# The early order of a fused attention and feed-forward kernel, laid out anew from the third scores to the first layer

## The chip, the cores and the metric

One core of a Trainium2 chip runs the kernel. The metric is the device time of one execution in microseconds; the median of three runs of the kernel before is 292.87 us (292.86 to 293.62).

## The reference

Inputs: `q`, `k`, `v` of 4 batches, 8 heads, 768 positions, 64 features; a projection to 6 hash bits; a norm gain; two weight matrices of 512 x 2048 and 2048 x 512.

```
q_bits = (einsum('bhsd,dk->bhsk', q, proj) > 0)
k_bits = (einsum('bhsd,dk->bhsk', k, proj) > 0)
mask = q_bucket[:, :, :, None] == k_bucket[:, :, None, :]
scores = where(mask, scale * q @ k^T, -1e9)
attn = softmax(scores)
x = (attn @ v), heads side by side: 4 x 768 x 512
xn = (x - mean(x)) / sqrt(var(x) + 1e-6) * g_ln
out = x + relu(xn @ w_ch1) @ w_ch2
```

## The kernel before

The work is cut into 12 units `u` of 256 query positions (three to a batch), and each unit into two groups `g` of 4 heads. A score block `s` is a unit, a group and a third of the keys (`kp`, 256 keys): `s = 6u + 3g + kp`, so there are 72.

Nothing is scheduled by a compiler. The string `ORDER` lists 1186 words; each word calls one function, and its second part names the engine that runs it: `t` TensorE (PE), `v` VectorE (DVE), `a` ScalarE (ACT), `p` GpSimd (POOL), `s` SyncE (SP, which issues most transfers). Each engine runs its words in the order of the string, and waits for what its operands and its buffers need. The string `SLOTS` names for each ring of buffers (a tag) which buffer each new tile takes, in the order in which tiles first appear; a new tile in a buffer must wait until the old one there has been read. The PSUM rings are `pp` (three buffers, for scores `sc` and for the sums `acc`) and `f` (two buffers, for everything else that PE writes).

The words that matter here, with the function's lines:

- `S.t.s` (L570): 24 small matmuls of one score block, 32 rows each, first the hash signs `G`, then the two halves of the features (`qb`, `kb`), into two `sc` tiles. `E.a.s.h` (L576): the exponential of half a block, 128 x 1024.
- `A.t.s` (L595): 16 matmuls of 65 columns, exponentials by values, added into `acc` of the unit and group. `na.v.u.g` (L608) reads `acc` when its three blocks are in; `nb` (L615, L617) divides; `nc`, `ag`, `ce` (L621 to L630) make the norm.
- For batch 0 the blocks of q and k are turned on DVE in thirds (`tn.v.g.t.kp`, L304; `t` is 0 for q, 1 for k), cast (`ca`, L311 to L315), hashed on PE (`ha`, L394, or by `hc`, `sl`, L405 and L418) and cut to signs (`bh`, `bc`, L307, `bi`, L428 and L430).
- For batch 1 and later a block of q or k is loaded by `LX.s.b.g.t` (L508) once `gx.p.b.g.t` (L505) has written one element of its buffer, a memset that stands for the wait until the buffer is free. `tu.v.b.g.t.n` (L304) turns a quarter of it, `CA` casts it, `hm.t.b.g` (L526) hashes all of q and k of a group once all eight `tu` are in, `bt` (L307) cuts to signs, and `mw` and `mr` (L544, L547) take them through DRAM.
- `ft.t`, `fc.v` (L644, L652) transpose unit 0's rows by PE and scale them. `F.t.u.p` (L659) is a first-layer block: 8 matmuls of 256 columns for two of the 16 hidden blocks. `R` (L667 on ACT, L669 on DVE) is its relu. `D.t` (L674) is the second layer of unit 0; later units use `P`, `Y` (L726, L731).
- `lw1.p.n`, `lw2.p.n` (L446, L457) load quarters of the weights from POOL; `lv.s`, `cv`, `su`, `sq`, `sp` bring in the values and their sums.

Of the kernel before, what the change touches and what calls it, by code (L numbers as in the profile page):

```python
# [43 lines left out]
sw.v.2.1 ce.v.1.0 fl.s.1.0 cv.p.1.0.0 wg.v.2 wg.a.0 D.t.0.1.0 ag.v.2.0 sw.v.4.1 ag.v.2.1
mr.s.1.1.0 E.a.18.1 mr.s.1.1.2 D.t.0.1.1 sw.v.1.1 D.t.0.0.2 cv.a.1.0.2 CA.a.1.1.0 S.t.20.2 E.a.20.1
lv.s.1.4.2 E.a.20.0 D.t.0.0.3 Z.v.0.0 D.t.0.1.2 D.t.0.1.3 Z.v.0.1 S.t.19.2 F.t.1.6 E.a.18.0
rs.p.2 F.t.1.3 CA.p.1.1.1 E.a.19.0 S.t.21.2 O.s.0.0 lv.s.1.4.1 E.a.19.1 A.t.19.2 E.a.21.0
R.v.1.6 sw.v.3.0 sw.v.2.0 E.a.21.1 F.t.1.0 R.a.1.0 lv.s.2.0.3 R.v.1.3 ce.v.2.1 sw.v.4.0
lv.s.1.4.0 ce.v.2.0 F.t.1.5 A.t.20.2 S.t.22.2 fl.s.2.1 tu.v.2.0.0.2 F.t.1.4 R.a.1.5 cv.p.1.4.0
# [740 lines left out]
```

## Time and profile before

| | us |
|---|---|
| median of three runs | 292.87 |
| the profiled execution, whole | 292.61 |
| its span, first to last instruction | 290.9 |
| DVE busy | 207.0 |
| ACT busy | 206.7 |
| POOL busy | 53.8 |
| granted TensorE clock | 1.0 throughout |

The profile is of one execution. Its views used below are the page (busy time, transfers by queue), busy time by stretch, the chain of waits (followed back from the last instruction: at each step what released it) and the timeline of single engines. A row of a timeline gives the start, the length, the engine, the line, what is written and read, the shapes, how many instructions are merged in it, and in brackets the idle time before it and what ended it. PE's matmuls are pipelined: one follows the last long before that one's end, so the length of a group is read from the next start.

### The profile page before, as it was taken

The numbers are of one execution on the slowest core, as the hardware profiler recorded it, in microseconds if no ns is written. First come the engines' busy times: TensorE is split into PE (matmuls) and PEld (weight loads), VectorE is DVE, ScalarE is ACT, GpSimd is POOL, SyncE is SP. The second block draws the span as 40 slices with busy tenths as digits, with TensorE's granted clock in tenths as the row PEclk, the third lists the DMA queues.
The fourth block names the chain that finished last, engine by engine and source line by source line (L and its number), as shares of the span: only waits on it lengthen the run. The fifth ranks groups of instructions, "written<-read, shape, count | busy, mean of one in ns | idle before, by whom it ended". The sixth has DMA issues, their size and how long they took to land.

```text
span 290.9 us, 10520 instructions
## 1 busy us (share of the span) xinstructions
PE 282.9 (97%) x4645; PEld 227.0 (78%) x4647; DVE 207.0 (71%) x478; ACT 206.7 (71%) x236; POOL 53.8 (18%) x88
## 2 busy tenths in 40 slices
PE   8998999999999999999999999999999999999994
PEld 4776777648788887888778878877888878898883
DVE  5758898896779795797667995876665655782653
ACT  4889998998966978784865996887794694515140
POOL 4560426232431005000300107210010010001000
PEclk9999999999999999999999999999999999999999
DMA  6999997646544591364430352220310301404022
GB/s 191 365 303 271 214 278 135 141 116 167 179 122 130 132 335 56 125 114 136 95 82 1 83 133 64 61 55 7 92 34 8 74 2 24 107 0 99 12 74 73
DMA packets 31055, 34.10 MB, mean 117 GB/s; under 512 B 15521, under 2 KB 27809, under 8 KB 31010
## 3 DMA queue, kind: packets, MB, share of 16 engines
q1 hardware_dynamic: 25938, 28.72, 35.3%
q0 software_dynamic: 4224, 4.19, 8.7%
q8 instruction: 36, 0.59, 0.9%
q10 hardware_dynamic: 848, 0.53, 0.7%
q14 instruction: 9, 0.07, 0.1%
HBM read 27.86 MB, written 6.88 MB: 119 GB/s over the span
## 4 chain that ended last, share of the span: by engine, by line
PE 95%; DVE 2%; ACT 1%; issue 1%; ACTq 0%; DVEq 0%
PE f L659 30%; PE sc L570 18%; PE X L726 13%; PE acc L595 13%; PE Yb L726 7%; PE Ya L726 3%; PE hp L526 3%; PE hf L394 3%; PE f L674 2%; PE warm L363 1%; ACT E L576 1%; DVE xnT L652 0%; PE hf L405 0%; PE vp L487 0%; PE Yc L726 0%
## 5 line engine op out<-in xcount | busy, mean ns | idle before, releaser
L576 ACT ACTIVATE E<-sc,bias_sb 128x1024 bf16<-128x1024 f32 x144 | 153.2, 1112 | 34.3 <-PE sc L570 31.1
L659 PE MATMUL f<-xnT,w_sb 128*128 128x256 bf16 x768 | 94.2, 273 | 0.2 <-DVE xnT L652 0.2
L659 PEld LDWEIGHTS <-w_sb 128*128 128x128 bf16 x768 | 71.5, 98 | 12.6 <-issue 5.0
L667 ACT ACTIVATE hb<-f 128x512 bf16<-128x512 f32 x67 | 39.7, 598 | 34.1 <-PE f L659 34.1
L570 PE MATMUL sc<-qb,kb 32*128 32x256 bf16 x1152 | 52.4, 267 | 0.0
L595 PE MATMUL acc<-vaug,E 128*128 128x65 bf16 x1152 | 43.9, 194 | 0.9 <-issue 0.9
L595 PEld LDWEIGHTS <-E 128*128 128x128 bf16 x1152 | 40.9, 98 | 5.0 <-issue 3.7
L570 PE MATMUL sc<-G 6*128 6x256 bf16 (+1 forms) x576 | 42.3, 273 | 0.9 <-ACT E L576 0.8
L726 PEld LDWEIGHTS <-hb 128*128 128x128 bf16 x352 | 33.4, 98 | 5.4 <-issue 1.3
L635 POOL TENSOR_SCALAR rs<-mv 128x2 f32<-128x2 f32 x12 | 3.3, 278 | 152.5 <-DVE mv L624 152.4
L570 PEld LDWEIGHTS <-kb 32*128 32x128 bf16 x1152 | 30.3, 93 | 1.5
L731 DVE TENSOR_TENSOR x<-X,x 128x256 f32<-128x256 f32 x44 | 18.4, 420 | 15.6 <-PE X L726 15.3
L570 PEld LDWEIGHTS <-G 6*128 6x128 bf16 (+1 forms) x576 | 15.8, 91 | 16.3 <-issue 13.5
L669 DVE TENSOR_SCALAR hb<-f 128x512 bf16<-128x512 f32 x29 | 19.8, 682 | 12.2 <-PE f L659 12.0
L726 PEld LDWEIGHTS <-S 128*128 128x128 bf16 x264 | 25.0, 98 | 4.5 <-issue 1.3
L304 DVE STREAM_TRANSPOSE T<-X 128x384 f32<-128x384 f32 (+2 forms) x52 | 26.1, 536 | 0.0
L608 DVE SCALAR_TENSOR_TENSOR y<-vsB,acc 128x520 f32<-128x520 f32 x24 | 16.6, 692 | 9.8 <-PE acc L595 9.5
L726 PE MATMUL Yb<-w_sb,S 128*128 128x256 bf16 x176 | 22.9, 273 | 0.0
L726 PE MATMUL X<-wt,hb 128*128 128x256 bf16 x168 | 21.8, 273 | 0.0
L621 DVE BATCH_NORM_STATS2 st<-x 128x6 f32<-128x256 f32 x48 | 17.4, 412 | 0.2
L617 DVE TENSOR_TENSOR x<-y,rc 128x512 f32<-128x512 f32 x24 | 16.6, 692 | 0.8
L731 DVE TENSOR_TENSOR x<-Yb,x 128x256 f32<-128x256 f32 x22 | 9.3, 421 | 9.7 <-PE Yb L726 9.5
(95 smaller groups left out, 266.4 us busy)
## 6 DMA issues: line engine op xcount, KB each, us to landing
out_dram<-x SPq DMA_DIRECT2D x45, 128.0 KB
X<-in_k_dram SPq DMA_DIRECT2D x7, 768.0 KB
vn<-in_v_dram SPq DMA_DIRECT2D x24, 192.0 KB
X<-in_q_dram SPq DMA_DIRECT2D x6, 768.0 KB
w_sb<-in_moe_w_ch_dram POOLq DMA_DIRECT2D x8, 512.0 KB, 11.7
vn<-in_v_dram SPq DMA_DIRECT2D x2, 768.0 KB
X<-in_q_dram SPq DMA_DIRECT2D x2, 512.0 KB
Bd<-B SPq DMA_DIRECT2D x6, 96.0 KB
```

The lines of the kernel that those rows point to most:

```text
L304: nc.vector.transpose(d[:, j], s[:, j, kj0 : kj0 + n])
L570: nc.tensor.matmul(sc(s, i // 2)[:, i % 2, 256 * kk : 256 * kk + 256], lh, rh, start=(rep == 0), stop=(rep == 2), skip_group_check=True,)
L576: nc.scalar.activation(E(s)[:, heads(h)], sc(s, h), AF.Exp, scale=EXP_SCALE, bias=bias_sb)
L595: nc.tensor.matmul(acc[:, qt, (D + 1) * i : (D + 1) * (i + 1)], E(s)[:, i, 256 * kk + P * qt : 256 * kk + P * qt + P], vaug(u // 3)[:, 4 * ...
L608: nc.vector.scalar_tensor_tensor(yt(u, g), vs, EPS_ROW, made[f"acc{u}{g}"][:, :, :A], op0=AOP.mult, op1=AOP.add,)
L617: nc.vector.tensor_tensor(xo, a[:, :, :, 0:D], rc.to_broadcast([P, 2, 4, D]), op=AOP.mult)
L621: nc.vector.bn_stats(stats(u)[:, qt, g], xt(u)[:, qt, 256 * g : 256 * g + 256])
L659: nc.tensor.matmul(f1[:, n].rearrange("p (t x) -> p t x", t=2), w1_sb[:, dt, P * nt : P * nt + P], xnT(u)[:, :, dt], start=(dt == 0), stop ...
L667: nc.scalar.activation(hb(u)[:, 2 * p : 2 * p + 2], f1, AF.Relu)
L669: eng.tensor_scalar_max(hb(u)[:, 2 * p : 2 * p + 2], f1, 0.0)
L726: nc.tensor.matmul(f2, lh[:, n], rh[:, n], start=(first and n == 0), stop=(n == 7), skip_group_check=True)
L731: nc.vector.tensor_tensor(x, made[f"{prod(u, k)}{u}"], x, op=AOP.add)
```

## The change

Only the strings change, not a function. The words are the same 1186. From `S.t.2.2` to `S.t.13.2` they stand in another order on TensorE, VectorE, ScalarE and GpSimd. From `S.t.13.2` on, TensorE has the same order as before; SyncE has the same order of transfers throughout. Farther down the words of one engine keep their order, and only their places among the words of other engines differ, which moves no instruction on its engine. In `SLOTS` the rings `E`, `X`, `f`, `pp` and `tp` change.

What moves, by engine:

- TensorE: `ha.1.1.0` goes ahead of `S.4`, `ha.1.1.2` behind `S.3`, `A.1` ahead of `S.3`, `hc.1.0.1` ahead of `S.8`; `A.3` comes ahead of `A.4` and `A.5`; `ft.0.0` ahead of `ft.0.1`; `hc.0.0.2` goes up to `S.9`, `F.0.3` down to `S.11`, `S.14` ahead of `hc.1.0.2`; `F.0.2` from behind `A.9` to between `A.11` and `A.10`.
- VectorE: the signs of `1.1.2` go behind `nb.0.0`; `nb.0.0`, `sc.0.4`, `tn.0.0.2` and the turns `tu.1.0.0.*` go forward, `tn.1.0.2`, `tu.1.0.1.1` to `tu.1.0.1.3` back; `wg.3` and `bt.1.0` go ahead of `CA.1.0.0`.
- ScalarE: halves of some blocks change places; `R.0.3` goes back with `F.0.3`, `ca.0.0.2` forward.
- GpSimd: `lw1.1` and `lw1.0` go ahead of `gx.1.0.1`, `cv.0.4.2` and `ca.1.1.2`; `gx.1.1.0` ahead of `lw2.0`; `CA.1.0.1` ahead of `rs.0`.
- Buffers: the loads of batch 1 sit in `X` buffers 0, 2, 1, 0 in place of 0, 2, 3, 1, so that the last of them (`gx.1.1.1`, `LX.1.1.1`) follows the turns of `X100`, and `gx.1.1.0` follows `tn.0.0.2`.

```
@@ -19,140 +19,140 @@
 p32.p tn.v.0.1.0 on.p.1 ca.a.0.0.0 pmem.p ha.t.0.0.0 bh.v.0.0.0 ha.t.0.1.0 bh.v.0.1.0 wm.t.2
 wm.t.3 ca.a.0.1.0 tn.v.0.1.1 ca.p.0.1.1 tn.v.0.1.2 S.t.0.2 E.a.0.0 E.a.0.1 ha.t.0.1.1 bh.v.0.1.1
 ha.t.0.1.2 bh.v.0.1.2 wm.t.6 tn.v.1.1.1 ca.p.1.1.1 lw1.p.3 ca.a.0.1.2 tn.v.1.1.0 S.t.1.2 E.a.1.1
-tn.v.1.0.0 ha.t.1.1.1 bh.v.1.1.1 cv.p.0.0.0 tn.v.1.1.2 gx.p.1.0.0 S.t.2.2 cv.p.0.0.2 cv.p.0.4.2 ca.p.1.1.2
-E.a.1.0 ca.a.1.0.0 lv.s.1.0.3 lw1.p.1 ha.t.1.0.0 bh.v.1.0.0 gx.p.1.0.1 LX.s.1.0.0 ha.t.1.1.2 bh.v.1.1.2
-E.a.2.1 lw1.p.0 ca.v.1.1.0 LX.s.1.0.1 tn.v.0.0.1 S.t.4.2 E.a.2.0 lv.s.1.0.2 ca.v.0.0.1 E.a.4.1
-ha.t.1.1.0 A.t.0.2 A.t.2.2 sq.t.0.0 E.a.4.0 bh.v.1.1.0 S.t.3.2 sc.v.0.0 A.t.1.2 cv.a.0.4.0
-E.a.3.1 hc.t.0.0.1 E.a.3.0 lw2.p.0 na.v.0.0 S.t.5.2 bc.v.0.0.1 sl.t.0.0.1 bi.v.0.0.1 E.a.5.1
-sq.t.0.4 tn.v.1.0.1 S.t.8.2 hc.t.1.0.1 nb.v.0.0 nc.v.0.0 E.a.5.0 bc.v.1.0.1 E.a.8.0 A.t.4.2
-A.t.5.2 sc.v.0.4 A.t.3.2 na.v.0.1 nb.v.0.1 E.a.8.1 sl.t.1.0.1 ca.a.1.0.1 bi.a.1.0.1 S.t.6.2
-gt.t E.a.6.0 nc.v.0.1 ag.v.0.1 S.t.7.2 ag.v.0.0 ce.v.0.1 ft.t.0.1 ce.v.0.0 gc.v
-E.a.6.1 E.a.7.0 ft.t.0.0 S.t.9.2 E.a.7.1 E.a.9.0 fc.v.0.1 E.a.9.1 fc.v.0.0 F.t.0.3
-A.t.7.2 R.a.0.3 F.t.0.7 R.a.0.7 S.t.10.2 tn.v.1.0.2 E.a.10.0 tu.v.1.0.1.2 gx.p.1.1.0 LX.s.1.1.0
-lw1.p.2 tu.v.1.0.1.3 tu.v.1.0.0.3 lv.s.1.0.1 E.a.10.1 tn.v.0.0.2 hc.t.0.0.2 ca.a.0.0.2 tu.v.1.0.1.0 A.t.6.2
-bc.v.0.0.2 sl.t.0.0.2 F.t.0.6 R.a.0.6 lw2.p.3 A.t.8.2 bi.v.0.0.2 S.t.11.2 F.t.0.0 tu.v.1.0.0.1
-hc.t.1.0.2 tu.v.1.0.1.1 gx.p.1.1.1 LX.s.1.1.1 na.v.1.0 tu.v.1.0.0.0 lw2.p.1 E.a.11.0 rs.p.0 tu.v.1.0.0.2
-R.v.0.0 E.a.11.1 CA.v.1.0.0 S.t.14.2 E.a.14.0 nb.v.1.0 bc.v.1.0.2 E.a.14.1 hm.t.1.0 ca.v.1.0.2
-lv.s.1.0.0 S.t.12.2 wg.v.3 sl.t.1.0.2 bi.a.1.0.2 bt.v.1.0 mw.s.1.0 mr.s.1.0.1 A.t.11.2 A.t.10.2
-tu.v.1.1.0.3 E.a.12.1 A.t.9.2 CA.p.1.0.1 na.v.1.1 nb.v.1.1 mr.s.1.0.2 mr.s.1.0.0 tu.v.1.1.0.1 tu.v.1.1.0.2
-E.a.12.0 nc.v.1.0 F.t.0.2 R.a.0.2 S.t.13.2 E.a.13.1 su.p.1.0 F.t.0.4 F.t.0.5 R.v.0.5
-S.t.16.2 lw2.p.2 E.a.13.0 A.t.12.2 E.a.16.0 A.t.13.2 A.t.14.2 tu.v.1.1.0.0 F.t.0.1 E.a.16.1
-tu.v.1.1.1.1 tu.v.1.1.1.3 R.a.0.4 na.v.2.0 tu.v.1.1.1.2 tu.v.1.1.1.0 nc.v.1.1 nb.v.2.0 R.a.0.1 S.t.15.2
...
+tn.v.1.0.0 ha.t.1.1.1 bh.v.1.1.1 cv.p.0.0.0 tn.v.1.1.2 gx.p.1.0.0 S.t.2.2 cv.p.0.0.2 lv.s.1.0.3 LX.s.1.0.0
+lw1.p.1 E.a.1.0 ca.a.1.0.0 ha.t.1.0.0 E.a.2.1 bh.v.1.0.0 E.a.2.0 lw1.p.0 ha.t.1.1.0 bh.v.1.1.0
+S.t.4.2 tn.v.0.0.1 ca.v.0.0.1 A.t.0.2 ca.v.1.1.0 E.a.4.1 gx.p.1.0.1 sq.t.0.0 E.a.4.0 cv.p.0.4.2
+LX.s.1.0.1 lv.s.1.0.2 cv.a.0.4.0 A.t.1.2 A.t.2.2 ca.p.1.1.2 S.t.3.2 sc.v.0.0 E.a.3.0 na.v.0.0
+nb.v.0.0 ha.t.1.1.2 bh.v.1.1.2 tn.v.1.0.1 hc.t.0.0.1 bc.v.0.0.1 S.t.5.2 E.a.3.1 E.a.5.0 sl.t.0.0.1
+sq.t.0.4 bi.v.0.0.1 tn.v.0.0.2 E.a.5.1 gx.p.1.1.0 lw2.p.0 hc.t.1.0.1 sc.v.0.4 LX.s.1.1.0 S.t.8.2
+E.a.8.0 A.t.3.2 A.t.4.2 bc.v.1.0.1 E.a.8.1 nc.v.0.0 A.t.5.2 na.v.0.1 nb.v.0.1 nc.v.0.1
+ag.v.0.0 ag.v.0.1 sl.t.1.0.1 bi.a.1.0.1 ce.v.0.0 S.t.6.2 lw1.p.2 ca.a.1.0.1 E.a.6.0 gt.t
+gc.v S.t.7.2 ft.t.0.0 E.a.6.1 lv.s.1.0.1 ce.v.0.1 ft.t.0.1 E.a.7.1 S.t.9.2 fc.v.0.1
+hc.t.0.0.2 E.a.7.0 E.a.9.0 A.t.7.2 fc.v.0.0 tu.v.1.0.0.2 F.t.0.7 tu.v.1.0.0.3 bc.v.0.0.2 E.a.9.1
+tu.v.1.0.0.0 A.t.6.2 S.t.10.2 R.a.0.7 A.t.8.2 tu.v.1.0.1.0 na.v.1.0 lw2.p.3 sl.t.0.0.2 F.t.0.3
+ca.a.0.0.2 tu.v.1.0.0.1 bi.v.0.0.2 E.a.10.1 E.a.10.0 R.a.0.3 S.t.11.2 E.a.11.1 F.t.0.6 R.a.0.6
+gx.p.1.1.1 E.a.11.0 F.t.0.0 tu.v.1.0.1.2 tn.v.1.0.2 S.t.14.2 E.a.14.1 nb.v.1.0 LX.s.1.1.1 lw2.p.1
+hc.t.1.0.2 lv.s.1.0.0 R.v.0.0 E.a.14.0 tu.v.1.0.1.3 tu.v.1.0.1.1 wg.v.3 hm.t.1.0 S.t.12.2 bc.v.1.0.2
+sl.t.1.0.2 bt.v.1.0 bi.a.1.0.2 CA.v.1.0.0 mw.s.1.0 mr.s.1.0.1 mr.s.1.0.2 ca.v.1.0.2 CA.p.1.0.1 mr.s.1.0.0
+mr.s.1.0.3 lv.s.1.4.3 A.t.11.2 F.t.0.2 A.t.10.2 tu.v.1.1.0.3 E.a.12.1 A.t.9.2 rs.p.0 na.v.1.1
+nb.v.1.1 tu.v.1.1.0.1 tu.v.1.1.0.2 E.a.12.0 nc.v.1.0 R.a.0.2 S.t.13.2 E.a.13.1 su.p.1.0 lw2.p.2
+F.t.0.4 F.t.0.5 R.v.0.5 S.t.16.2 E.a.13.0 A.t.12.2 E.a.16.0 A.t.13.2 A.t.14.2 tu.v.1.1.0.0
...
-    E="012302132023132032103230103231032031230120302123031230120321013202120320",
+    E="012301203130203103210301210302103102301231013230102301231032120313231031",
-    X="0123023120312032",
-    f="10010101010101010101010100101010101001010111101010010100100101010111010101010101000010010101001001011000001011010101110101010101110101010111010101010111010101011",
+    X="0123021032103213",
+    f="01010101010101001101011011010101010110101000010101101011011010101000101010101010111101010101001001011000001011010101110101010101110101010111010101010111010101011",
-    pp="0121020102011202102102102121021020212012012012112012010121021202012010201202101202102010202120212110201101002120102102101210021202120102100210210102010201012102102120210",
+    pp="0121020102012012012012102110201020212012012012112012010121021202012010201202101202102010202120212110201101002120102102101210021202120102100210210102010201012102102120210",
-    tp="012102101201210210210210210120210210210120120",
+    tp="012012010210210210210210210120210210210120120",
```

More of the change, by code (lines that the diff above doesn't have):

```diff
@@ L44 @@
[L44 to L49, printed above, removed]
@@ new lines @@
+R.a.0.1 S.t.15.2 E.a.15.0 nc.v.2.0 ag.v.1.0 E.a.15.1 hm.t.1.1 S.t.17.2 D.t.0.0.0 sw.v.3.1
+E.a.17.0 ag.v.1.1 rs.p.1 bt.v.1.1 mw.s.1.1 LX.s.2.0.0 mr.s.1.1.3 D.t.0.0.1 wg.v.1 A.t.16.2
+A.t.15.2 E.a.17.1 A.t.17.2 na.v.2.1 nb.v.2.1 S.t.18.2 ce.v.1.1 fl.s.1.1 mr.s.1.1.1 nc.v.2.1
+sw.v.2.1 ce.v.1.0 fl.s.1.0 mr.s.1.1.0 mr.s.1.1.2 lv.s.1.4.2 cv.p.1.0.0 wg.v.2 wg.a.0 D.t.0.1.0
+ag.v.2.0 sw.v.4.1 ag.v.2.1 E.a.18.1 D.t.0.1.1 sw.v.1.1 D.t.0.0.2 cv.a.1.0.2 CA.a.1.1.0 S.t.20.2
+E.a.20.1 E.a.20.0 D.t.0.0.3 Z.v.0.0 D.t.0.1.2 D.t.0.1.3 Z.v.0.1 O.s.0.0 lv.s.1.4.1 lv.s.2.0.3
@@ new lines @@
+E.a.29.1 S.t.28.2 E.a.28.1 E.a.28.0 R.v.2.4 ag.v.3.1 hm.t.2.0 bt.v.2.0 mw.s.2.0 lv.s.2.4.2
+O.s.1.3 O.s.1.2 S.t.31.2 F.t.2.0 R.v.2.0 E.a.31.1 E.a.31.0 F.t.2.5 R.a.2.5 rs.p.3
+ce.v.3.0 fl.s.3.0 S.t.27.2 E.a.27.0 E.a.27.1 ce.v.3.1 fl.s.3.1 LX.s.3.1.1 lv.s.2.4.1 LX.s.2.1.1
+mr.s.2.0.2 LX.s.3.0.1 mr.s.2.0.0 O.s.1.1 mr.s.2.0.3 mr.s.2.0.1 F.t.2.2 F.t.2.7 A.t.28.2 cv.v.2.0.2
+A.t.29.2 tu.v.2.1.0.1 nb.v.4.0 R.v.2.7 S.t.30.2 A.t.27.2 tu.v.2.1.0.2 cv.a.2.0.0 CA.v.2.0.1 R.a.2.2
+E.a.30.0 F.t.2.3 R.a.2.3 P.t.2.2 na.v.4.1 nb.v.4.1 S.t.32.2 F.t.3.6 E.a.30.1 A.t.30.2
@@ new lines @@
+lv.s.3.4.1 O.s.2.3 S.t.38.2 F.t.3.5 R.v.3.0 A.t.34.2 R.a.3.5 F.t.3.3 CA.v.2.1.1 R.a.3.3
+tu.v.3.0.1.0 E.a.38.1 A.t.35.2 F.t.3.4 A.t.33.2 nb.v.5.0 F.t.3.1 R.a.3.4 na.v.5.1 tu.v.3.0.0.3
+F.t.3.2 E.a.38.0 R.a.3.1 rs.p.4 ce.v.4.1 fl.s.4.1 S.t.36.2 P.t.3.2 R.a.3.2 E.a.36.1
+nb.v.5.1 su.p.2.4 ss.v.3.1 Y.v.3.2 P.t.3.1 E.a.36.0 S.t.39.2 E.a.39.1 E.a.39.0 ce.v.4.0
+fl.s.4.0 LX.s.3.1.0 Y.v.3.1 nc.v.5.0 A.t.37.2 P.t.3.5 ss.v.3.2 ss.v.3.4 A.t.36.2 Y.v.3.5
+cv.v.2.4.0 P.t.3.6 Y.v.3.6 P.t.3.3 A.t.38.2 ss.v.3.3 S.t.40.2 Y.v.3.3 E.a.40.0 E.a.40.1
@@ L125 @@
+A.t.69.2 P.t.9.2 Y.v.9.2 ss.v.9.4 P.t.9.1 E.a.70.0 Y.v.9.1 A.t.70.2 na.v.11.1 nb.v.11.1
 F.t.10.7 P.t.9.6 R.a.10.7 Y.v.9.6 nc.v.11.0 P.t.9.5 P.t.9.7 Y.v.9.5 Y.v.9.7 nc.v.11.1
```

126 lines of the change are left out of this document (57 added, 69 removed).

## The prediction

> **What bounds the kernel now.** I read the page first, then busy time by stretch, then the chain of waits and the timelines of single engines between 18 and 46 us, because the order of work on TensorE, VectorE, ScalarE and GpSimd differs only up to `S.13`.
>
> ```profile
> span 290.9 us, 10520 instructions
> ...
> PE 282.9 (97%) x4645; PEld 227.0 (78%) x4647; DVE 207.0 (71%) x478; ACT 206.7 (71%) x236; POOL 53.8 (18%) x88
> ...
> q8 instruction: 36, 0.59, 0.9%
> ```
>
> ```profile
> 26.00:46.00 20.00, 18.50 (x426) 14.48 (x423) 17.56 (x42) 18.32 (x22) 7.02 (x10) 1.00 1.11 238
> ...
> 57.30:290.90 233.60, 229.27 (x3640) 187.89 (x3638) 162.86 (x357) 157.64 (x182) 30.57 (x42) 1.00 0.34 88
> ```
>
> The columns of the second view are stretch, length, then busy time of PE, PEld, DVE, ACT and POOL. From 57.30 on PE is busy for 229.27 of 233.60 us, in an order that the change leaves alone, and the renamed buffers follow each other there as before. So the time moves by as much as the start of `S.13` moves (45.21 now). Between 26 and 46 us PE, DVE and ACT are all near full (18.50, 17.56 and 18.32 of 20) and the DMA share is 1.11: here a wait on one engine quickly becomes a wait of another.
>
> PE has few holes there. The chain of waits (start, length, what) shows two with no releaser, both in the middle of a run of value products:
>
> ```profile
> 25.39 0.35 issue
> 25.75 0.40 PE acc L595 x7
> ...
> 35.42 0.12 PE hf L418 x4
> ...
> 36.41 0.49 PE acc L595 x16
> ...
> 38.64 0.36 PE hf L405 x16
> ...
> 39.77 1.44 PE hp L526 x32
> 41.21 0.77 PE sc L570 x24
> ...
> 43.30 0.56 issue
> 43.86 0.54 PE acc L595 x12
> 44.40 0.88 PE f L659 x8
> ```
>
> I take them for waits on PE's own program. The page's instruction queue moved 0.59 MB in 36 packets; PE's 4645 + 4647 instructions give 258 to a packet. Counting the order (a product is a load and a multiply: `S` 48 instructions, `A` 32, `F` 16, `hc` 32, `hm` 64), the first hole lies at PE instruction 700, in `A.3`, and the second at 1466, in `A.9`: 766 apart, three packets of 255. The transfers by queue, in 23.4:24.5, 29.3:30.5 and 41:42.4, each hold one such packet:
>
> ```profile
> q8 instruction: 1, 0.02, 5.4%
> ...
> q8 instruction: 1, 0.02, 4.4%
> ```
>
> PE goes on at 25.75 and 43.86, 1.25 and 1.46 us behind the end of the first and the last stretch. So a packet asked for at one edge (PE passed 444 in `hc.0.0.1`, the row at 19.89 below, and 1211 in `hc.1.0.2`, 38.7) is usable 5.1 to 5.9 us later, and 255 instructions of only scores and value products, 80 in 0.77 + 0.49 us, are through sooner. First-layer blocks (16 in 0.88) are slow in instructions and give it time.
>
> The Trainium skill, "Runtime: NRT & Kernel Launch", section "Instruction fetch mechanics", has refills in 16 KiB blocks of 256 instructions, which agrees with 0.59 MB / 36, but calls the cost of a block's edge "mostly hidden". Holes of 0.35 and 0.56 us beyond a matmul's own 0.19 in the pipeline, so start steps of 0.55 and 0.75 where 0.49/16 = 0.03 is usual, speak against that here; its result is the second rival.
>
> **Part 1: third scores to the first transposes** (`S.2` to `ft`). On PE `ha.1.1.2` goes behind `S.3`, `A.1` ahead, `hc.1.0.1` ahead of `S.8`, `A.3` to `A.5` change places. On DVE `bh.1.1.2` moves behind `nb.0.0`.
>
> ```profile
> 13.20 1.92 PE hf L394 x8
> ...
> 19.89 0.43 PE L405 MATMUL hf<-tp,p 128*32 128x64 f32 x16
> 20.65 0.38 PE L570 MATMUL sc<-G 32*128 32x256 bf16 x4 [0.33 <-ACT E L576]
> ...
> 26.18 0.29 PE L570 MATMUL sc<-G 32*128 32x256 bf16 x4
> ...
> 30.22 0.35 PE L570 MATMUL sc<-G 32*128 32x256 bf16 x4
> ...
> 27.11 6.14 ACT L576 ACTIVATE E<-sc,bias_sb 128x1024 bf16<-128x1024 f32 x6 [0.45 <-PE sc L570]
> ```
>
> `S.5` starts at 20.65 now and needs the moved signs. Laid out with the rows, the hash product (1.92/2 = 0.96 us) follows `S.3` from 18.8, and the DVE pass over 256 columns (0.43, row at 35.57 below) follows that: 20.5. An exponential takes 6.14/6 = 1.02, so both of `S.5` are through near 23.5, and `A.3`, `A.4` and ten products of `A.5` reach instruction 700 at 24.8, earlier than now (25.2). The packet's request (edge 444, in `hc.0.0.1`, 19.89) is not earlier, since the work ahead of it is the same in sum and PE does not wait long there. So PE again goes on at 25.75, `S.6` starts at 26.2 and, through its exponentials, `S.9` at 30.2 as now (26.18, 30.22). Value of part 1: 0. Bounds: without the fetch, the exponential of `S.8` lets `S.6` go at 25.6 (-0.6); a packet 1 us later costs +1.0.
>
> **Part 2: loads.** GpSimd now issues `lw1.1` and `lw1.0` ahead of the casts, and the buffer table lets `gx.1.1.0` follow `tn.0.0.2`, which moves forward; `gx.1.1.1` follows `tu.1.0.0.1`, since its buffer is now that of `X100`.
>
> ```profile
> 31.98 0.10 POOL L505 MEMSET X<- 128x1 f32 x1 [11.25 <-DVE tp L304]
> ...
> 32.11 0.33 SPq L508 DMA_DIRECT2D X<-in_q_dram  x1
> 34.14 0.33 SPq L508 DMA_DIRECT2D X<-in_k_dram  x1
> ...
> 43.62 1.81 POOL L480 TENSOR_TENSOR t<-vn 128x768 f32<-128x768 f32 x1 [5.15 <-DMA vn<-in_v_dram]
> ```
>
> The 11.25 us wait of POOL goes, and with it weights `lw1.2` and `lw2.3` and the SP load at 32.11 start some 9 us sooner. No PE row waits for them, so that gains nothing. The load at 34.14 goes to about 36.1; behind it on SP stand `lv.1.0.0` and `mw.1.0`, on POOL `lw2.1`. Its block is first turned by `tu.1.1.1.1` near 49: 13 us for a transfer, covered. `su.1.0` (43.62) may start 2 us later, and the last weights behind it too; they serve `D.0.0.2` at about 60, covered. Value 0; the bound above is the extra DMA load between 23 and 32 us, where the share is already over 1 and an instruction packet must get through (first rival).
>
> **Part 3: from `S.9` to the hash product `hm.1.0`.** Rows for the durations, DVE timeline:
>
> ```profile
> 29.96 1.29 DVE L652 TENSOR_TENSOR xnT<-ft,gT 128x512 bf16<-128x512 bf16 x2
> 31.16 0.76 DVE L304 STREAM_TRANSPOSE tp<-X 128x256 f32<-128x256 f32 x2
> 31.85 1.46 DVE L304 STREAM_TRANSPOSE T<-X 128x384 f32<-128x384 f32 x3
> ...
> 35.57 0.43 DVE L430 CAST G<-hf 128x256 bf16<-128x256 f32 x1 [0.46 <-PE hf L418]
> ...
> 36.94 0.70 DVE L608 SCALAR_TENSOR_TENSOR y<-vsB,acc 128x520 f32<-128x520 f32 x1
> ...
> 38.68 0.69 DVE L669 TENSOR_SCALAR hb<-f 128x512 bf16<-128x512 f32 x1
> ...
> 40.16 0.20 DVE L615 RECIPROCAL rc<-y 128x8 f32<-128x8 f32 x1
> 40.39 0.69 DVE L617 TENSOR_TENSOR x<-y,rc 128x512 f32<-128x512 f32 x1
> ```
>
> PE: `S.9` at 30.2; `hc.0.0.2` needs the buffer that `fc.0.1` reads: 31.1; `A.7` 31.5, `F.7` 32.0, `A.6` 32.9; `S.10` needs the sixth exponential (27.11 + 6.14 = 33.25): 33.5; `A.8` 34.3 to 34.75. A result reaches DVE 0.2 us after PE, so `na.1.0` starts at 34.95. DVE has done its `fc` and four `tu` by 33.7 and waits 1.2 us: what is queued behind `na.1.0` are the last turns for `hm`. They run: `na` 0.61 (starts follow 0.61 apart), `tu` 0.49, `bi` 0.34, `tu` 0.49, `tn` 0.69, `nb` 0.87, to 38.45. `R.0.0` needs `F.0.0`, which PE reaches through `sl`, `F.3` (0.88), `S.11` (0.77), `F.6` at 37.5 and ends at 38.4: `R` 38.6, then 0.61 + 0.49 + 0.54 + 0.05 to PE. `hm.1.0` starts at **40.25**. PE itself would be ready at 39.5 (`S.14` 0.77 and `hc` 0.36 behind `F.0.0`). Now it starts at 39.70 with the turns done 1.1 earlier:
>
> ```profile
> 39.70 1.51 PE L526 MATMUL hp<-T,p 128*32 128x192 f32 x32
> ```
>
> Term: **+0.55**. Bounds: 0 to +0.9 (a `tu` or the `R` wait more or less).
>
> **Part 4: `F.0.2` between `A.11` and `A.10`.**
>
> ```profile
> 44.24 1.04 PE L659 MATMUL f<-xnT,w_sb 128*128 128x256 bf16 x8
> 45.21 0.29 PE L570 MATMUL sc<-G 32*128 32x256 bf16 x4
> ...
> 44.44 0.69 DVE L608 SCALAR_TENSOR_TENSOR y<-vsB,acc 128x520 f32<-128x520 f32 x1 [0.89 <-PE acc L595]
> ```
>
> It takes the second hole away: instruction 1466 is now in `A.10`, reached at 44.3, while the packet (edge 1211 in `S.14`, 38.7, plus 5.1) is there at 43.8. Term **-0.75**. But the block was the cover of another wait. `S.13` writes into the PSUM buffer of `acc11`, which `na.1.1` must have read: 44.44 + 0.70 + 0.05 = 45.2, just when `F.0.2` ended. With `F.0.2` gone from there, `A.9` is followed at once by `S.13`: 0.2 + 0.70 + 0.05 = 0.95 of wait, where entering `S` costs 0.1 anyway: **+0.85**. Check: `hm` 40.25 + 1.44, `S.12` 0.77, `sl` 0.12, `A.11` 0.49, `F.2` 0.88, `A.10` and `A.9` 0.98 end at 44.93; `S.13` at 45.88 against 45.21.
>
> **Sum.** 0.55 - 0.75 + 0.85 = +0.65. The profiled execution took 292.61 (span 290.9, 1.7 around it): 293.26. The median of the runs is 0.26 above the profiled one: **293.5**.
>
> **Rivals.** *Slower: an instruction packet comes late.* The edge at 956 is reached in `A.7` at 31.9; now it lies a block later, in `F.7`. The packet in 29.3:30.5, plus 1.3, is usable at about 31.75: a margin of 0.15, and beside it now runs the advanced `X` load. From there each microsecond is one at the end, since `S.10`, `A.8`, `na.1.0` and `hm` follow; the same holds at 700 and, behind 0.5 of margin, at 1466. For it: three margins, two of them thin, in a stretch with a DMA share over 1. Against: the packets waited beside the same weights before. At a lateness of 0.9: 294.4.
>
> *No hole recurs.* If packets come early enough, or the holes were something else, `S.6` starts at 25.6, `hm` at 39.45 and `S.13` at 45.1: 292.7. The skill's rule above would give this. Against: the edge and its request lie where they did.
>
> *Faster.* That, and `S.13` not held by `na.1.1` (-0.85 more): 292.0 or a little less. For it: in before the end of `F.0.2` and the release fall together, so the trace doesn't show which of them held `S.13`. Against: the table gives `sc131` the buffer of `acc11`.
>
> **How the numbers follow.** A measurement here tells about 0.3% (0.9 us) from no change: 292.0 and 293.75 are the bounds. My forecast has 0.44, by itself 292.9 to 294.0, of which 0.13 lies above 293.75; the late packet 0.30; no hole 0.16; faster 0.10. So faster 0.10, same 0.31 + 0.16 = 0.47, slower 0.43. The range 292.2 to 294.8 takes in the first two bounds of parts 1 and 3 and a packet late by 1.3.
>
> **What would show it.** A hole with no releaser in `A.5`, ending near 25.7, and none in `A.10` or `A.9`; `S.6` at 26.2; PE idle before `hm.1.0` until DVE's turns end, with `hm` near 40.25; DVE waiting for `acc` before `na.1.0`; PE idle about 0.85 before `S.13`, released by `na.1.1`; `S.13` near 45.9 and everything behind it moved by the same 0.65. I am wrong if `S.6` starts more than 0.3 from 26.2, if `hm` starts before 39.8, or if PE has new holes behind 57 us.

## The result and the profile after

The changed kernel takes 294.61 us (median of 15 runs, 293.14 to 295.13) against 292.87 (15 runs, 291.67 to 293.66): ratio 1.0051, 95% interval 1.0037 to 1.0065, so about 1.5 us slower. The page of its profiled execution, and busy time in the same first stretch as before and in the stretch from `S.18` on:

```profile
span 292.9 us, 10521 instructions
...
PE 284.4 (97%) x4647; PEld 227.9 (78%) x4647; DVE 209.2 (71%) x478; ACT 206.0 (70%) x236; POOL 54.8 (19%) x88
```

```profile
26.00:46.00 20.00, 18.57 (x427) 14.80 (x424) 16.29 (x37) 18.27 (x23) 5.31 (x8) 1.00 1.11 246
59.32:292.90 233.58, 229.34 (x3641) 187.92 (x3638) 162.77 (x357) 157.53 (x182) 31.28 (x42) 1.00 0.33 88
```

Behind `S.18` nothing has changed: 233.58 us against 233.60. The 2.0 us between the two spans lie ahead of it. Of the list of TensorE's waits up to 62 us, the lines of 0.3 us or more that only one of the two kernels has, before and then after:

```profile
PE acc L595 <- issue: 0.9, 2, 0.6
...
PE ft L644 <- DVE xc L628: 0.3, 1, 0.3
```

```profile
PE hf L418 <- DVE Bc L307: 0.8, 1, 0.8
PE sc L570 <- DVE y L608: 0.6, 1, 0.6
PE sc L570 <- DVE kb L315: 0.6, 1, 0.6
...
PE sc L570 <- DVE G L307: 0.3, 1, 0.3
```

Columns: engine and tile that wait, engine and tile waited for, us in total, times, longest. Both holes without a releaser ("issue") are gone, and in their place stand four waits for VectorE. The chain of waits of the changed kernel shows two of them, those behind `S.12`:

```profile
40.23 0.94 DVE T L304 x2
41.18 0.98 DVE w_sb L454 x2
42.16 0.64 issue
42.80 0.61 DVE w_sb L454 x2
43.41 0.15 DVE Bc L307
...
43.60 0.28 PE hf L418 x4
43.88 0.49 PE acc L595 x16
44.37 0.87 PE f L659 x8
45.24 0.99 PE acc L595 x32
...
46.25 0.71 DVE y L608
```

At 43.60 `sl.1.0.2` (`hf` L418) starts 0.83 us later, counted from the end of `S.12`, than before: `bc.1.0.2` (`Bc`), which used to run ahead of the four products of `wg.3` (`w_sb` L454), now stands behind them, and the four together take twice as long. (The list of moves ahead of the prediction leaves this move out, and also that `ca.1.1.0` goes behind `tn.0.0.1` and `ca.0.0.1`, which run 9 takes up.) At 46.25 `na.1.1` holds `S.13`, as Part 4 had it. VectorE's timeline after and before, and GpSimd's at the same place, after and before:

```profile
41.10 2.31 DVE L454 TENSOR_SCALAR w_sb<-w_sb,gT 128x512 bf16<-128x512 bf16 x4
43.34 0.21 DVE L307 TENSOR_SCALAR Bc<-hf 128x64 bf16<-128x64 f32 x1
```

```profile
41.00 0.22 DVE L307 TENSOR_SCALAR Bc<-hf 128x64 bf16<-128x64 f32 x1
...
41.46 1.14 DVE L454 TENSOR_SCALAR w_sb<-w_sb,gT 128x512 bf16<-128x512 bf16 x4
```

```profile
41.24 1.49 POOL L315 CAST kb<-T 128x1536 bf16<-128x1536 f32 x1 [2.82 <-DVE T L304]
```

```profile
37.01 1.47 POOL L315 CAST kb<-T 128x1536 bf16<-128x1536 f32 x1 [1.10 <-DVE T L304]
```

GpSimd's cast `CA.1.0.1` needs the turns `tu.1.0.1.*`. The change moved the last of them to just ahead of `wg.3`, so the cast starts with the products. In the chain the third product starts at 42.80, 0.07 behind the cast's end (41.24 + 1.49). The same four products one by one (count, then shortest, median and longest in ns), after and before:

```profile
L454 DVE TENSOR_SCALAR w_sb<-w_sb,gT x4: 311/344/1553, 41.1 to 43.1; 128x512 bf16<-128x512 bf16 x4
```

```profile
L454 DVE TENSOR_SCALAR w_sb<-w_sb,gT x4: 346/347/348, 41.5 to 42.2; 128x512 bf16<-128x512 bf16 x4
```

So not every product is slow: one of them, the second (41.33 to 42.88), takes 1.55 us and ends 0.15 behind the cast, and the other three take what they took before.

**A common zero.** Up to `S.2` the order is the same in every kernel here, yet `S.2` starts anywhere from 11.90 to 13.47 us in the fourteen profiles below (11.90 to 12.61 in the four with the order before, 11.98 to 13.47 in the ten with the changed one). The start of TensorE's work, before and after, shows where that arises:

```profile
4.30 0.59 PE L366 MATMUL warm<-ones 128*128 128x512 bf16 x2
4.73 1.89 PE L394 MATMUL hf<-tp,pfull 128*128 128x256 f32 x8
```

```profile
4.50 1.06 PE L366 MATMUL warm<-ones 128*128 128x512 bf16 x2
5.35 2.24 PE L394 MATMUL hf<-tp,pfull 128*128 128x256 f32 x8
```

Two products on ones that fill the wait for data take 0.43 us to the next start in one execution and 0.85 in the other. TensorE's first products of 512 columns follow each other every 0.43 us, and from some moment on every 0.21. In the traces the record of the granted clock (at 1.0) starts at that moment: at 4.09 us before and 6.05 with the change, and over the fourteen from 3.86 (run 8) to 7.06 (run 4). The later it lies, the later `S.2` starts, without exception, and it lies ahead of every word whose place differs. So 0.80 of the 2.0 us between the profiles (`S.2` at 12.16 and 12.96) is the draw of the execution. From here on starts are counted from the first product of `S.2`, each read from TensorE's timeline of that run. A row shows one execution, which need not be a usual one: in runs 5 and 11 it was the fastest of twelve (292.19 where the median is 293.79, and 292.22 where it is 293.14).

| kernel | ratio, 95% | `S.2` at | `S.5` | `S.12` | `sl.1.0.2` | `S.16` | `S.18` | `S.12` to `S.18` |
|---|---|---|---|---|---|---|---|---|
| before | 1 | 12.16 | 8.49 | 28.98 | 29.74 | 35.66 | 45.14 | 16.16 |
| changed | 1.0051, 1.0037–1.0065 | 12.96 | 9.27 | 29.05 | 30.64 | 36.65 | 46.36 | 17.31 |
| 1 bias first | 1.0061, 1.0039–1.0084 | 12.46 | 9.40 | 29.18 | 29.95 | 36.75 | 46.46 | 17.28 |
| 2 block alone (on before) | 1.0001, 0.9982–1.0019 | 12.61 | 8.49 | 28.68 | 29.44 | 35.60 | 45.09 | 16.41 |
| 3 block back | 1.0028, 1.0011–1.0044 | 12.34 | 9.34 | 29.12 | 30.71 | 36.05 | 45.76 | 16.64 |
| 4 cast off GpSimd | 1.0044, 1.0028–1.0061 | 13.47 | 9.29 | 29.07 | 29.83 | 36.12 | 45.82 | 16.75 |
| 5 products later | 1.0040, 1.0025–1.0056 | 11.98 | 8.41 | 28.21 | 28.97 | 35.21 | 44.91 | 16.70 |
| 6 and cover | 1.0028, 1.0010–1.0046 | 13.27 | 9.29 | 29.07 | 29.83 | 35.15 | 45.38 | 16.31 |
| 7 before and cover | 1.0006, 0.9991–1.0020 | 12.52 | 8.50 | 28.45 | 29.22 | 34.53 | 44.54 | 16.09 |
| 8 numbers shifted (on before) | one run | 11.90 | 8.49 | 28.45 | 29.21 | 34.97 | 44.78 | 16.33 |
| 9 cast order back | 1.0056, 1.0037–1.0075 | 13.20 | 8.40 | 28.18 | 29.77 | 35.79 | 45.49 | 17.31 |
| 10 three edits | 1.0020, 1.0007–1.0033 | 13.05 | 9.08 | 28.86 | 29.62 | 34.91 | 45.14 | 16.28 |
| 11 ScalarE number | 1.0014, 0.9999–1.0028 | 12.05 | 8.96 | 28.73 | 29.50 | 34.68 | 44.69 | 15.96 |
| 12 casts ahead of loads | 1.0004, 0.9990–1.0019 | 13.03 | 8.47 | 28.25 | 29.02 | 34.20 | 44.41 | 16.16 |

### The profile page after: what moved, and what is told of

Same layout as the page of the kernel before. It is cut to its first block, busy times and chain, and to the rows that moved or that the text cites. A ratio compares the mean times of both kernels' runs of the same rounds, so it can differ in the third digit from the quotient of the medians.

```text
span 292.9 us, 10521 instructions
## 1 busy us (share of the span) xinstructions
PE 284.4 (97%) x4647; PEld 227.9 (78%) x4647; DVE 209.2 (71%) x478; ACT 206.0 (70%) x236; POOL 54.8 (19%) x88
## 4 chain that ended last, share of the span: by engine, by line
PE 92%; DVE 4%; ACT 1%; issue 1%; DVEq 0%
PE f L659 29%; PE sc L570 18%; PE X L726 13%; PE acc L595 11%; PE Yb L726 7%; PE Ya L726 3%; PE f L674 2%; PE hp L526 2%; PE hf L394 2%; ACT E L576 1%; PE warm L363 1%; DVE w_sb L454 1%; DVE y L608 0%; DVE kb L315 0%; DVE qb L313 0%
## 5 line engine op out<-in xcount | busy, mean ns | idle before, releaser
L570 PE MATMUL sc<-G 6*128 6x256 bf16 (+1 forms) x576 | 43.1, 273 | 1.6 <-DVE y L608 0.6
L595 PEld LDWEIGHTS <-E 128*128 128x128 bf16 x1152 | 40.9, 98 | 4.3 <-issue 2.9
L595 PE MATMUL acc<-vaug,E 128*128 128x65 bf16 x1152 | 43.7, 194 | 0.2 <-ACT E L576 0.2
```

The source lines that it names most:

```text
L570: nc.tensor.matmul(sc(s, i // 2)[:, i % 2, 256 * kk : 256 * kk + 256], lh, rh, start=(rep == 0), stop=(rep == 2), skip_group_check=True,)
L595: nc.tensor.matmul(acc[:, qt, (D + 1) * i : (D + 1) * (i + 1)], E(s)[:, i, 256 * kk + P * qt : 256 * kk + P * qt + P], vaug(u // 3)[:, 4 * ...
```

## The experiments

**1. Bias first.**

```
-wg.v.3 hm.t.1.0 S.t.12.2 bc.v.1.0.2 sl.t.1.0.2
+bc.v.1.0.2 wg.v.3 hm.t.1.0 S.t.12.2 sl.t.1.0.2
```

> The changed order with one word moved: the copy of the hashes bc.1.0.2 stands on VectorE ahead of the four products of wg.3 instead of behind them. Measured from the first product of S.2 (profile of the changed kernel: sl.1.0.2 at 30.64, F.0.4 at 34.80; of the one before: 29.74 and 33.81). Theory (the products of wg.3 take 2.31 us because GpSimd's cast CA.1.0.1 runs beside them, and sl.1.0.2 pays for it): sl.1.0.2 at 29.8, right behind S.12, F.0.4 at 34.0, and 0.8 us of the whole time comes back (ratio to the kernel before 1.002). Rival 1 (the loss is the start of the kernel, not this place): sl.1.0.2 is as early, but the ratio stays at 1.005. Rival 2 (sl.1.0.2 has another wait right behind, the buffer of the hashes or TensorE's instruction packet): sl.1.0.2 stays at 30.4 or later. In all four runs the start of S.2 is looked at: if the 0.80 by which it was late is chance, it lies anywhere from 12.1 to 13.0, if it belongs to the changed order, it is 12.9 in the three kernels with that order and 12.2 in the fourth.

`sl.1.0.2` came back to 29.95, but nothing was gained: `S.16` at 36.75. The wait went one word further on TensorE. VectorE's timeline, and the wait that is new in the list of waits:

```profile
40.85 2.44 DVE L454 TENSOR_SCALAR w_sb<-w_sb,gT 128x512 bf16<-128x512 bf16 x4
43.21 0.54 DVE L307 TENSOR_SCALAR B<-hp 128x384 bf16<-128x384 f32 x1
```

```profile
PE f L659 <- DVE B L307: 0.6, 1, 0.6
```

`F.0.2` takes the PSUM buffer of `hp`, which `bt.1.0` (`B`) must have read, and `bt.1.0` still stands behind the products. The theory missed this second reader; the slow products were not yet tested. Here the product that waits is the first (1.64 us), though its record starts 0.03 ahead of the cast's.

**2. Block alone.**

```
 (the kernel before)
-A.t.11.2 A.t.10.2 ... A.t.9.2 ... nc.v.1.0 F.t.0.2 R.a.0.2 S.t.13.2
+A.t.11.2 F.t.0.2 A.t.10.2 ... A.t.9.2 ... nc.v.1.0 R.a.0.2 S.t.13.2
```

> The kernel before with one word moved: F.0.2 between A.11 and A.10, and nothing else of the change. Theory of the prediction: the hole at TensorE instruction 1466 (0.75) is gone and a wait of 0.85 for na.1.1 comes ahead of S.13: F.0.4 at 33.9 from the first product of S.2 (33.81 before), whole time +0.1 us, ratio 1.000. Rival (the release by na.1.1 is not what held S.13): no wait at S.13, F.0.4 at 33.1, ratio 0.997. Rival (the hole belongs to the place and not to the instruction's number, or the packet is later): hole still there beside the new wait, F.0.4 at 34.7, ratio 1.003.

The chain of waits of this kernel:

```profile
42.83 1.00 PE f L659 x8
43.84 0.99 PE acc L595 x32
...
44.85 0.71 DVE y L608
...
45.60 0.83 PE sc L570 x22
```

The 32 products of `A.10` and `A.9` run in 0.99 without a hole, and `S.13` waits for `na.1.1`. From `sl.1.0.2` on `F.0.4` comes after 4.31 us (33.75 - 29.44) against 4.07 (33.81 - 29.74); the time is the same. Hole and wait change places, as the prediction had it.

**3. Block back.** The changed kernel with `F.0.2` behind `A.9` again.

> The changed order with one word moved: F.0.2 behind A.9 again, as before the change. Theory (in the changed kernel everything is late enough that the packet with TensorE's instruction 1466 is there, usable from about 44.5, when A.9 asks for it at 44.7): no hole, no wait of 0.85 ahead of S.13, F.0.4 at 34.0 from the first product of S.2 (34.80 with the change), time -0.8 us, ratio 1.002. Rival (the hole comes back): 0.75 for 0.85, F.0.4 at 34.7, ratio 1.005. sl.1.0.2 stays at 30.6 in both.

`F.0.4` at 34.20, `S.16` 0.60 earlier, ratio 1.0028; the wait list has no `y` and no "issue" in the value products. In this run no hole is met at instruction 1466, so beside the slow products the moved block pays for the wait it exposes and gets nothing back: 0.60 of the loss. The two losses are not independent: the wait of `sl.1.0.2` lies between 1211 and 1466. TensorE gets there 5.2 us behind 1211, where before it had got there after 4.5 and then waited until 5.2. Whether the hole comes back with the products out of the way and the block where it was, no run tests.

**4. Cast off GpSimd.**

```
-CA.p.1.0.1 ... rs.p.0 ... su.p.1.0
+CA.v.1.0.1 ... su.p.1.0 rs.p.0
```

> The changed order with CA.1.0.1 on VectorE instead of GpSimd, behind wg.3, and GpSimd's two short operations rs.0 moved behind su.1.0: nothing runs on GpSimd beside wg.3, while bc.1.0.2 still stands behind wg.3. Theory (two engines at one port): the four products of wg.3 take 1.15 us again instead of 2.31, bc.1.0.2 runs at 42.2 to 42.4, sl.1.0.2 right behind S.12, 29.8 from the first product of S.2, time -0.8 us, ratio 1.002, unless the extra 0.95 us on VectorE makes na.1.1 late (then 1.003 to 1.005). Rival (the products were slow because VectorE waited for its own instructions, the packet that ended at 43.24, or for the weights): 2.2 to 2.3 us as before, sl.1.0.2 at 30.6, ratio 1.005.

VectorE's timeline of this kernel:

```profile
41.63 1.10 DVE L454 TENSOR_SCALAR w_sb<-w_sb,gT 128x512 bf16<-128x512 bf16 x4
42.64 0.21 DVE L307 TENSOR_SCALAR Bc<-hf 128x64 bf16<-128x64 f32 x1
```

With GpSimd idle the same four products, in the same place, on the same weights, take 1.10 us, and `sl.1.0.2` follows `S.12` at once. That settles the cause of the 0.83. (The Trainium skill, "SBUF — State Buffer", section "SBUF: two separate sides", says that VectorE and GpSimd share one pair of ports, and that of a GpSimd instruction and a VectorE instruction that takes the pair, whichever starts first keeps it to its end and the other is blocked. The changed kernel's one product of 1.55 us, which ends 0.15 us behind the cast, agrees; which came first can't always be read from the starts, as run 1 shows.) `S.18` moves by 0.54; the ratio, 1.0044, can't be told from 1.0051, and 1.002 was expected.

**5. Products later.** `wg.v.3` behind `wg.v.1`, and nothing else of the changed order.

> The changed order with one word moved: the four products of wg.3 go from ahead of bc.1.0.2 to behind wg.1, some 15 us later, where nothing runs on GpSimd; F.1.6, the first block that reads this quarter scaled, comes later still. Theory (both waits that the products cause, the one of sl.1.0.2 for bc.1.0.2 and the one of F.0.2 for bt.1.0, go together; TensorE's instruction packet no longer binds there): sl.1.0.2 at 29.8 from the first product of S.2, F.0.2 at 30.4, then the wait of 0.85 for na.1.1, F.0.4 at 34.0 to 34.3 (34.80 with the change), ratio 1.002 to 1.003. Rival (another release behind the first two holds F.0.2 or A.10 as well, as bt.1.0 did in the first run of this series): F.0.4 at 34.7 or later, ratio 1.005.

From `S.12` to `S.18` 16.70 instead of 17.31, which is the gain of run 4 (16.75), here without another word in the way. `S.18` at 44.91 is not to be taken for the edit's worth: this execution, the fastest of its twelve, also had `S.5` at 8.41, of which more under run 9. The ratio, 1.0040, lies above the 1.002 to 1.003 expected.

**6. And cover.** Run 5, with `F.t.0.4` ahead of `S.t.13.2`.

> The run before this one, and F.0.4 put ahead of S.13 as the cover for the wait for na.1.1 (0.88 of work for 0.85 of wait). Theory: S.16, 36.65 from the first product of S.2 with the change and 36.0 in the run before this one, starts at 35.2; before it was 35.66. The ratio is 0.999 to 1.001. Rival (the wait moves on: S.13's exponentials start 0.05 to 0.9 later and S.16, A.12 or A.13 wait for them): S.16 at 35.2, but S.15 (38.87 before) no earlier than 39.2, ratio 1.002 to 1.003.

`S.16` came at 35.15 as expected, but half was given back: `A.12` now waits for the exponentials of `S.13`, and `S.15` stands at 38.89 (38.87 before). Ratio 1.0028: the rival's, though it had `S.15` no earlier than 39.2.

**7. Before and cover.** The kernel before, `F.0.2` between `A.11` and `A.10`, `F.0.4` ahead of `S.13`.

> The kernel before with two first-layer blocks moved and nothing else: F.0.2 between A.11 and A.10, F.0.4 ahead of S.13. Theory (block between the value products: no hole at instruction 1466, -0.75; block ahead of S.13: the wait for na.1.1 is covered): S.16 at 34.9 from the first product of S.2 (35.66 before), ratio 0.997. Rival (the gain is given back at S.15, S.17 or the exponentials behind S.13): S.18 within 0.2 of 45.14, ratio 1.000. Rival (the hole comes back at another place): S.16 at 35.6, with a stretch of TensorE without a releaser in it.

No hole, no wait for `na.1.1`, `S.16` at 34.53, `S.18` 0.60 earlier than in the profile of before. The times don't show it: 1.0006. Of the 0.60, 0.53 lies ahead of `S.12` (28.45 against 28.98), where the order is the same: the profile of before had a hole of 0.35 at instruction 700, which runs 7 and 8 did not have. Counted from `S.12`, `S.16` comes 0.60 sooner (6.08 against 6.68), but `S.15` at 9.82 against 9.89 and `S.18` at 16.09 against 16.16: as in run 6, what is won ahead of `S.13` is given back by `S.15`. That is the first rival.

**8. Numbers shifted.** The kernel before; the 13 warm-up products of 512 columns are each written as two of 256.

```
-for _ in range(NWARM): matmul(wp[:, 0], ones, row(4, P))
+for i in range(2 * NWARM): matmul(wp[:, 0, 256 * (i % 2) : 256 * (i % 2) + 256], ones, row(2, P))
...
```

> The kernel before, with each warm-up product of 512 columns written as two of 256: 13 products more at the start (26 instructions more), the same work, order and waits behind it. Theory (the holes stand at fixed instruction numbers, 700 and 1466, where a packet of the program ends): both come 13 products earlier. The second leaves 25 value products behind it instead of 12, so it falls into A.10 with 9 of its 16 products to come; the first leaves 20 instead of 7, if S.2 starts early enough for it to be there at all. Rival (the holes belong to their place, by a wait or a memory that the trace does not show): 12 and 7 products behind them as before.

The chain of waits of this kernel (its lines are one higher: L596 is L595):

```profile
41.40 0.70 PE acc L596 x23
42.11 0.40 issue
42.51 0.95 PE acc L596 x25
```

25 products behind the hole instead of 12: it moved by exactly the 13 that were put in at the start, 40 us ahead. This hole belongs to an instruction number. The one at 700 does not appear in this execution.

**9. Cast order back.**

```
-tn.v.0.0.1 ca.v.0.0.1 A.t.0.2 ca.v.1.1.0
+ca.v.1.1.0 tn.v.0.0.1 ca.v.0.0.1 A.t.0.2
```

> The changed order with one word moved: VectorE's cast ca.1.1.0 goes back ahead of the transposes tn.0.0.1, where it stood before the change; it then runs before GpSimd's casts cv.0.4.2 and ca.1.1.2 begin and not beside them. Theory (the same meeting of the two engines as at wg.3): the cast takes 0.64 us instead of 1.48 and ca.0.0.1 0.7 to 1.2; S.3 waits for nothing; S.5 starts at 8.5 to 8.7 from the first product of S.2 (9.27 with the change), S.12 at 28.4 to 28.7 (29.05), the wait for bc.1.0.2 stays, F.0.4 at 34.2 to 34.5 (34.80), ratio 1.003. Rival (the place saves nothing, since TensorE's packet with instruction 700 sets S.6): S.5 early, but S.6 at 13.9 to 14.1, S.12 at 29.0, ratio 1.005.

VectorE's casts at this place, before and then with the change, and GpSimd's with the change:

```profile
15.51 0.64 DVE L315 CAST kb<-tp 128x512 bf16<-128x512 f32 x1
...
16.86 0.72 DVE L313 TENSOR_SCALAR qb<-tp 128x512 bf16<-128x512 f32 x1
```

```profile
17.10 1.23 DVE L313 TENSOR_SCALAR qb<-tp 128x512 bf16<-128x512 f32 x1
18.25 1.48 DVE L315 CAST kb<-tp 128x512 bf16<-128x512 f32 x1
```

```profile
17.20 0.84 POOL L475 CAST vaug<-vn 128x768 bf16<-128x768 f32 x1
17.96 1.30 POOL L315 CAST kb<-tp 128x512 bf16<-128x512 f32 x1
```

In this run the casts took 0.78 and 0.75, `S.5` came at 8.40 and `S.12` at 28.18, but the ratio stayed at 1.0056. One profile is not enough here: in run 10, with the same word moved, the same casts took 1.22 and 1.30, and in run 5, without it, 1.24 and 0.43. Which engine comes first is decided by tenths of a microsecond and differs between executions. Alone, the edit is not shown to help.

**10. Three edits.** Runs 6 and 9 together.

> The changed order with three words moved: ca.1.1.0 as in the run before this one, wg.3 behind wg.1, F.0.4 ahead of S.13. Theory (what the change lost, it lost where VectorE and GpSimd meet, and ahead of S.13): S.12 at 28.4 to 28.7, S.16 at 34.5 to 34.8 (35.66 before the change, 36.65 with it), S.18 at 44.7 to 45.0 (45.14, 46.36), ratio 0.998 to 1.000. Rival (there is a further loss behind 57 us that the first products don't show): S.18 as above, but a ratio of 1.003 or more.

`S.12` at 28.86 and `S.18` at 45.14, each some 0.15 us above what was expected, with VectorE's casts at 1.22 and 1.30. The ratio, 1.0020, gives back 0.9 of the 1.5 us, less than the 0.998 to 1.000 expected.

**11. ScalarE number.** Run 10, with `nc.scalar.activation(junk, bias_sb, AF.Exp)` written twice.

> The run before this one, with one more instruction of 0.2 us at the start of ScalarE (the exponential that loads the table is written twice). Theory (ScalarE's stretch of 0.32 to 0.37 us without a releaser between the semaphore and the exponential E.15.0, seen in all runs of the changed order and not in those of the order before, is the edge of a packet at a fixed instruction number): with the number moved by one, E.15.0 starts within 0.1 of its semaphore, S.17 takes 0.77 instead of 0.98, S.18 0.2 earlier than in the run before this one. Rival (the stretch belongs to E.15.0 itself): it stays at 0.32 or more, S.17 at 0.95 to 1.0.

ScalarE's timeline of the changed kernel and of this one, at `E.15.0`:

```profile
54.09 2.12 ACT L576 ACTIVATE E<-sc,bias_sb 128x1024 bf16<-128x1024 f32 x2 [0.52 <-PE sc L570]
```

```profile
51.40 4.33 ACT L576 ACTIVATE E<-sc,bias_sb 128x1024 bf16<-128x1024 f32 x4 [0.22 <-PE sc L570]
```

One instruction more at the start takes the late start of `E.15.0` away (0.52 of idle time to 0.22; 0.18 before the change), and `S.17` takes 0.77 instead of the changed kernel's 0.99. Against run 10, which differs by this instruction alone, the idle time falls from 0.56 to 0.22 and `S.17` from 0.88. So the stall hangs on the instruction number, and an edge of ScalarE's program is the reading that fits. Ahead of `E.15.0` the changed order has the same fifty words on ScalarE and, in the trace, one wait for a semaphore more.

**12. Casts ahead of loads.**

```
 (run 11)
-cv.p.0.0.2 lw1.p.1 lw1.p.0 gx.p.1.0.1 cv.p.0.4.2 ca.p.1.1.2
+cv.p.0.0.2 cv.p.0.4.2 ca.p.1.1.2 lw1.p.1 lw1.p.0 gx.p.1.0.1
```

> The run before this one, with GpSimd's casts cv.0.4.2 and ca.1.1.2 ahead of its two issues of weights lw1.1 and lw1.0, as before the change. In that run VectorE's cast ca.0.0.1 still took 1.77 us beside GpSimd, S.5 started at 8.96 from the first product of S.2, S.12 at 28.73, S.18 at 44.69. Theory (what is left of the loss between S.2 and S.6 is the meeting of ca.0.0.1 with GpSimd's casts, which the advanced issues brought under it): ca.0.0.1 takes 0.4 to 0.8 us, S.5 at 8.4 to 8.5, S.12 at 28.2 to 28.3, S.18 at 44.1 to 44.3, ratio 0.998 to 1.000. Rival (the casts wait for their data, not for the issues, and meet ca.0.0.1 wherever they stand): 1.2 to 1.8 us again, S.5 at 8.9 to 9.1, S.18 at 44.6 to 44.8, ratio 1.001.

VectorE's casts of this kernel, and then GpSimd's:

```profile
16.38 0.62 DVE L315 CAST kb<-tp 128x512 bf16<-128x512 f32 x1
...
17.71 1.30 DVE L313 TENSOR_SCALAR qb<-tp 128x512 bf16<-128x512 f32 x1
```

```profile
16.45 1.25 POOL L475 CAST vaug<-vn 128x768 bf16<-128x768 f32 x1 [0.63 <-DMA X<-in_q_dram]
17.65 1.08 POOL L315 CAST kb<-tp 128x512 bf16<-128x512 f32 x1
```

The same two of run 11, VectorE's second cast and GpSimd's:

```profile
16.73 1.77 DVE L313 TENSOR_SCALAR qb<-tp 128x512 bf16<-128x512 f32 x1
```

```profile
17.13 1.09 POOL L315 CAST kb<-tp 128x512 bf16<-128x512 f32 x1
```

`S.5` and `S.12` came as the theory had them, `S.18` 0.1 later, though the cast `ca.0.0.1` still took 1.30 and not 0.4 to 0.8. It starts 4.68 us behind `S.2` in both runs and ends 0.28 behind the end of GpSimd's second cast in both; GpSimd's cast ends 0.47 sooner here (5.70 behind `S.2` instead of 6.17), and that is the 0.49 of `S.5`. So the casts still meet, and the issues decide for how long. `ca.1.1.0`, 0.07 ahead of GpSimd's first cast, took 0.62 (0.63 in run 11); here it was GpSimd's that took longer, 1.25 instead of 0.83. With this the changed order is back at 1.0004 (0.9990 to 1.0019); run 11 had 1.0014, and the intervals overlap. None of the versions is shown to be faster than the kernel before.

## Why the prediction was right or wrong

The forecast was 293.5 us, +0.65, most likely within 0.3%; the kernel lost 1.5. Its 294.61 us lie inside the stated range (292.2 to 294.8) and, by the prediction's own bound of 293.75, count as slower, which had 0.43 against 0.47. That the range held is in part luck: its upper end was drawn for an instruction packet that comes late, and the time went elsewhere. Taking as the usual value before the mean of the four profiles with that order (before, 2, 7, 8) and after that of the six with the changed one up to `S.12` (changed, 1, 3 to 6), `S.12` starts at 28.64 and at 28.95: +0.31. From `S.12` to `S.18` the profiles of before and after differ by 17.31 - 16.16 = 1.15. Together 1.46, against 1.5 by the ratio. The 1.15 is made up of 0.83 (`S.12` to `sl.1.0.2`), 0.09 (`sl.1.0.2` to `F.0.4`) and 0.23 (`F.0.4` to `S.18`).

- **The step that failed** is the check at the end of Part 4: "`hm` 40.25 + 1.44, `S.12` 0.77, `sl` 0.12". The term for `sl` should have been 0.12 + 0.83. The working followed `hm`'s turns through VectorE, but not `bc.1.0.2`, which the change puts behind `wg.3`, and it took each operation at the length it had before, where GpSimd did nothing beside it. Run 4 shows that the four products take their old time when GpSimd is idle, run 1 that the next reader behind them is late too.
- **Part 1**, value 0: `S.6` is at 14.04 against 14.02 from `S.2`, and yet the reason was false. No hole stood in `A.5`. `S.3` waited 0.6 for a cast that took 1.48 us (0.64 before), which the laying-out of rows did not have, and `S.5` 0.3 for its signs; instruction 700 was then passed without a hole. Against profiles of the order before that had no hole either (runs 7 and 8: `S.6` at 13.50) this costs 0.5.
- **The packet.** That holes stand at instruction numbers is shown by run 8 for the second. That a packet is usable 5.1 to 5.9 us after the edge that asks for it fits there but not at the first. By the traces' records TensorE goes on at 1466 5.19 us behind 1211 before and 5.37 in run 8; in runs 4, 5, 6 and 10 a start step of 0.14 to 0.29 is left within two instructions of that number, ending 5.20 to 5.36 behind. But at 700 it goes on 5.84 behind 444 before, 5.54 in run 2, and run 9 passes there without a hole after 4.89. What sets the packet's time stays open. "Mostly hidden", as the Trainium skill has it ("Runtime: NRT & Kernel Launch", section "Instruction fetch mechanics"), does not hold for the 0.40 of run 8 and the 0.30 (0.52 - 0.22) that run 11 took off ScalarE. It does for most edges: before, TensorE's list of waits has two such holes in the whole span, for 36 packets.
- **Part 2**, 0: true of the transfers, for which no matmul waited. Not of the two issues on GpSimd, which pushed its casts: run 12 against run 11 gave 0.49 at `S.5` and 0.28 at `S.18` in one profile of each; the times do not separate the two.
- **Part 3**, +0.55: `hm.1.0` started at 27.49 from `S.2`, 27.54 before, and waited for nothing ahead of it. That is 39.65 on the clock of before, under the 39.8 that the prediction named as a sign of being wrong. DVE's wait for `na.1.0` came as laid out (1.62 us). But I took `hm` for one piece that needs all eight turns. It hashes q first; the last turn of k (40.64 to 41.18) came while it ran (from 40.45). From `S.9` to `S.12` the change cost 0.17.
- **Part 4**, -0.75 + 0.85: confirmed in both halves by run 2, and +0.09 in the changed kernel (`sl.1.0.2` to `F.0.4`: 4.16 against 4.07), where `S.13` takes 1.61 us instead of 0.77, close to the 0.85 of the forecast. But beside the slow products the hole would not have been met there any more (run 3), so in their company the move cost 0.60.
- **Not foreseen**: the late start of `E.15.0` on ScalarE, 0.22 on `S.17` against before, of which run 11 against run 10 shows 0.11.
- **Rivals.** "An instruction packet comes late" named 294.4, close to the time, by a mechanism that is not there: TensorE has no stretch without a releaser in the changed kernel's list of waits. Its thin margin of 0.15 was a miscount: by the records of the traces instruction 956 starts at 33.1 us before, in `F.0.7`, and at 32.9 with the change, in `A.7`, not at 31.9. "No hole recurs" was right about the holes and wrong about what follows. "Faster" had `S.13` not held by `na.1.1`; run 2 shows that it is.
